# Window attention and two MLP layers: four phases over all tokens, seven block products in place of eight

## The chip, the cores and the metric

One core of one Trainium2 chip runs the whole program. The metric is the time of one execution on the device, in microseconds (us).

## The reference

Attention with 8 heads of 64 over 4 sequences of 576 tokens: each token sees itself and the 127 before it, with a linear bias per head. Its output is turned into 2304 rows of 512 and goes through two MLPs with 2048 hidden values each; the first gates with h tanh(softplus(h)) (Mish), the second with ELU.

```python
scores = scale * np.matmul(q, k.transpose(0, 1, 3, 2))
mask = (rel >= 0) & (rel < window)
scores = np.where(mask, scores + bias[None], -1000000000.0)
attn = np.exp(scores - np.max(scores, axis=-1, keepdims=True))
attn = attn / (np.sum(attn, axis=-1, keepdims=True) + 1e-09)
x = np.ascontiguousarray(np.matmul(attn, v).transpose(0, 2, 1, 3)).reshape(B * S, H * D)
h = x @ w_in                                      # layer 1
x = (h * np.tanh(np.log1p(np.exp(h)))) @ w_out
h = x @ w_in2                                     # layer 2
out = np.where(h > 0.0, h, np.exp(h) - 1.0) @ w_out2
```

Weights arrive as 64-bit floats and are made 32-bit on the chip.

## The kernel before, in words

**Products.** Every product of the layers is a sum of three products of rounded values: an operand x is split into hi (x rounded to fp32r, a copy, L411) and lo (x - hi, rounded, L421), and hi*hi + hi*lo + lo*hi are added up in one PSUM bank.

**Layer 1** runs over chunks of 512 tokens (the first in halves of 256 columns; the last 64 tokens of the four sequences form one chunk of 256). For each of 16 blocks of 128 hidden values, `hidden1` makes 12 products (L773) into a bank `ph`; Mish is taken in place (L782), split into gh and gl, and `output1` adds 12 products (L814) into banks `py`, which hold the chunk's result over all 16 blocks. The result goes to DRAM (`x2_scratch`). All weights of layer 1 stay on chip, split; those of layer 2 take their places while the last layer-1 chunk runs. **Layer 2** is the same with `hidden2` (L935), the exponential and two DVE steps for ELU (L945, L946, L948), and `output2` (L967).

**Attention** is 48 units: 4 sequences, 4 pairs of heads, 3 parts (row blocks 0 and 1; 2 and 3; the tail of 64 rows). A unit makes scores (L559 in plain fp32 for 12 units, L562 and L564 from split q and k for most others, L569 for tails), masks them (L580), takes the row maximum and the exponential (L583, L587), normalises (L603), transposes (L628), masks again (L644, L653) and multiplies with v (L679), two heads side by side in the output's partitions. Attention of the next sequence runs among the products of the current chunk.

**Weights** (`load_weights`): per 512 columns one load, two ACT and two DVE instructions and one POOL addition (L470 to L481) make 32-bit values, then hi and lo.

**What sets the order.** The program is written as a list of operations with due times; `Plan.order` walks through them with a table of costs, gives each engine the most urgent operation whose operands and buffers are ready, and may choose between ACT, DVE and POOL for copies, subtractions and scalings. The engines then run that fixed order. Where PE would wait early in the program, it puts in unused products (L349). All bulk transfers go out on the SP queue.

Of the kernel before, what the change touches and what calls it, by code (L numbers as in the profile page):

```python
# [13 lines left out]
AT = dict(lag=2, step=6.96, late=25.76, copy=1.19, both=0.34, conv=-34.61, conv1=8.2, mish=-3.26, out=-0.67,
          prep=-6.85, load=-27.75, loadr=12.24, unit=3.02, unit1=3.1, split=6.31, x2=-21.79, w2=1.86, step2=1.49,
          g=-8.44, stage=-21.52, fill=170.0, enough=1.5, u0=0.0, u1=5.67, t0=1.26, t1=11.22, t2=4.45, u2=33.61, u3=4.87,
          norma=0.5, normp=8.33, relt=-15.35, d00=-2.11, d01=-2.85, d10=0.27, d11=1.21, dx=3.28, plain=6.14,
          mm2=8.39, first=-1000.0, second=-53.57, wadd=1.47, whi=-10.73, wlo=9.29, norm=-2.13, mask=-3.68, gl=13.52,
          newton=-9.59, elu=-24.7, lead=1, turn=2.71, held=28.54, k0=8, k1=0, u4=0.0, u5=5.67)

SHIFT = dict(H18=24.6, H21=-8.7, H3=18.1, H4=12.6, H5=6.8, H69=-11.9, H7=38.3, H71=-16.6, H8=-27.9, I3=-54.8, I4=-16,
             O16=86.4, O18=56.7, O19=-34.6, O2=13.6, O4=-9.9, O5=51.4, O66=46.4, O7=19, O70=63.2, O8=-77.9, O9=35.1,
             P29=-68.1, e2=9.8, g1=-37.5, g19=-11.3, g2=-10.4, g6=-22.6, g69=1, g7=5.3, g8=104.2, u0000=-105.9,
             u0001=-69.1, u0010=-40.7, u0011=-16, u0100=-145.3, u0101=-117.5, u0102=-152.8, u0103=-153.5,
             u010l=-127.6, u0110=-11.6, u0112=11.3, u011l=-13.4, u0121=-44.7, u0122=-3.4, u012f=32.3, u012l=-77.8,
             u0131=22.6, u0201=-22.8, u0210=-9.7, u1001=3.7, u100l=-19.2, u1010=-22.3, u1011=-40.4, u101l=-24.9,
             u1020=-135.2, u1021=-51, u1022=-27.9, u1030=9, u103f=20.8, u1100=38.6, u1101=-22.4, u1103=28.6,
             u1110=-97, u1111=-137.2, u1112=-163.5, u1120=-59.6, u1121=-90.6, u1131=10.4, u1133=15.3, u113c=-62.7,
# [1021 lines left out]
```

## Time and profile before

| | us |
|---|---|
| median of 3 runs | 938.47 (935.89 to 940.75) |
| span of the profiled execution | 939.7 |
| PE busy | 924.6 (98%) |
| DVE busy | 519.1 (55%) |
| ACT busy | 499.7 (53%) |
| POOL busy | 172.6 (18%) |

The span runs from the first to the last instruction of the profiled execution; it lies inside the range of the three runs, and no other time of that execution is given. A PE duration holds the way through the array, so products of a row overlap and their starts tell the rate. A DVE or ACT duration also runs a little into the next one's when one follows at once.

### The profile page before, as it was taken

How to read it: one execution, taken by the hardware profiler on the slowest of the kernel's cores; microseconds unless marked ns; L12 is line 12 of the kernel's file. 1: busy time of each engine (PE TensorE's matmuls, PEld its weight loads, DVE VectorE, ACT ScalarE, POOL GpSimd, SP SyncE). 2: the span in 40 equal slices, each digit the busy share in tenths (PEclk: the TensorE clock that was granted, in tenths of full speed). 3: DMA queues.
4: the chain of work that ended last, by engine and by line, in shares of the span. 5: the costliest groups of instructions: out<-in, count | busy, mean ns of one | idle time of the engine just before them, and what ended most of it. 6: DMA issues, size and time to landing. Idle time of an engine off the chain costs nothing.

```text
span 939.7 us, 13784 instructions
## 1 busy us (share of the span) xinstructions
PE 924.6 (98%) x5095; PEld 773.1 (82%) x5095; DVE 519.1 (55%) x1309; ACT 499.7 (53%) x1018; POOL 172.6 (18%) x151
## 2 busy tenths in 40 slices
PE   8989999999999999999999999999999999999998
PEld 5778889987888787799888888888888888888897
DVE  6878889866524367851566894343334333333333
ACT  4888988875726567872677773233223222322232
POOL 1553455511100001010465462000000000000000
PEclk9999999999999999999999999999999999999999
DMA  9335455243202123440544440011001000100010
GB/s 218 120 127 168 161 166 173 86 126 114 86 1 85 43 65 96 130 155 13 155 146 155 149 157 24 0 45 45 1 1 56 12 1 1 45 1 0 1 46 23
DMA packets 32387, 75.08 MB, mean 80 GB/s; under 512 B 5696, under 2 KB 12352, under 8 KB 32320
## 3 DMA queue, kind: packets, MB, share of 16 engines
q1 hardware_dynamic: 31792, 73.55, 25.1%
q10 hardware_dynamic: 528, 0.66, 0.3%
q8 instruction: 40, 0.66, 0.3%
q14 instruction: 27, 0.22, 0.1%
HBM read 64.23 MB, written 9.96 MB: 79 GB/s over the span
## 4 chain that ended last, share of the span: by engine, by line
PE 88%; ACT 4%; DVE 3%; DMA 2%; POOL 1%; issue 1%; SPq 0%; POOLq 0%
PE ph L935 21%; PE py L967 21%; PE py L814 19%; PE ph L773 19%; PE ps_o L679 3%; DMA raw<-in_w_dram 2%; PE ps_t L628 1%; PE ps_s L559 1%; PE ps_s L564 1%; PE ps_s L562 1%; POOL bits L481 1%; ACT p L587 1%; ACT raw L476 1%; ACT raw L473 1%; PE ps_s L569 1%
## 5 line engine op out<-in xcount | busy, mean ns | idle before, releaser
L421 DVE TENSOR_TENSOR gl<-ph,gh 128x512 fp32r<-128x512 f32 (+1 forms) x152 | 100.3, 660 | 161.1 <-ACT gh L411 160.5
L935 PE MATMUL ph<-x,wih 128*128 128x512 f32 (+1 forms) x640 | 181.8, 367 | 0.0
L411 ACT ACTIVATE gh<-ph 128x512 fp32r<-128x512 f32 (+1 forms) x142 | 81.1, 573 | 132.5 <-PE py L967 122.9
L773 PE MATMUL ph<-xh,wih 128*128 128x256 f32 (+1 forms) x384 | 134.4, 350 | 3.6 <-DVE gl L421 3.3
L935 PEld LDWEIGHTS ph<-x,wih 128*128 128x128 f32 x640 | 117.5, 188 | 22.6 <-DVE gl L421 0.2
L814 PE MATMUL py<-gh,woh 128*128 128x256 f32 (+1 forms) x384 | 135.1, 352 | 0.0
L814 PE MATMUL py<-gh,wol 128*128 128x256 f32 (+1 forms) x384 | 129.6, 337 | 1.1 <-POOL wol L421 0.9
L773 PE MATMUL ph<-xl,wih 128*128 128x256 f32 (+1 forms) x384 | 129.8, 338 | 0.7 <-DVE xl L421 0.7
L814 PE MATMUL py<-gl,woh 128*128 128x256 f32 (+1 forms) x384 | 129.5, 337 | 0.3 <-DVE gl L421 0.3
L773 PE MATMUL ph<-xh,wil 128*128 128x256 f32 (+1 forms) x384 | 129.5, 337 | 0.0
L935 PE MATMUL ph<-x,wil 128*128 128x512 f32 (+1 forms) x320 | 117.6, 368 | 0.0
L945 ACT ACTIVATE e<-ph 128x512 f32<-128x512 f32 (+1 forms) x80 | 44.4, 555 | 132.8 <-PE ph L935 131.9
L967 PE MATMUL py<-woh,gh 128*128 128x512 f32 x288 | 112.4, 390 | 0.0
L967 PE MATMUL py<-woh,gl 128*128 128x512 f32 x288 | 112.3, 390 | 0.0
L967 PE MATMUL py<-wol,gh 128*128 128x512 f32 x288 | 112.1, 389 | 0.0
L481 POOL TENSOR_TENSOR bits<-bits,raw 128x512 int32<-128x512 int32 x64 | 87.6, 1371 | 99.6 <-DVE bits L478 72.4
L946 DVE TENSOR_SCALAR e<-e 128x512 f32<-128x512 f32 (+1 forms) x80 | 33.3, 416 | 113.6 <-ACT e L945 113.6
L773 PEld LDWEIGHTS ph<-xh,wih 128*128 128x128 f32 x384 | 73.1, 190 | 15.6 <-DVE gl L421 4.1
L814 PEld LDWEIGHTS py<-gh,wol 128*128 128x128 f32 x384 | 72.8, 190 | 9.4 <-POOL wol L421 1.1
L814 PEld LDWEIGHTS py<-gh,woh 128*128 128x128 f32 x384 | 72.8, 190 | 8.5 <-issue 1.5
L773 PEld LDWEIGHTS ph<-xl,wih 128*128 128x128 f32 x384 | 73.2, 191 | 7.9 <-DVE xl L421 0.9
L773 PEld LDWEIGHTS ph<-xh,wil 128*128 128x128 f32 x384 | 73.1, 190 | 7.8
(104 smaller groups left out, 1499.5 us busy)
## 6 DMA issues: line engine op xcount, KB each, us to landing
raw<-in_w_dram SPq DMA_DIRECT2D x64, 512.0 KB, 4.3
qkv<-in_qkv_dram SPq DMA_DIRECT2D x12, 640.0 KB, 4.0
qkv<-in_qkv_dram SPq DMA_DIRECT2D x16, 288.0 KB, 2.9
x_scratch<-ys SPq DMA_DIRECT2D x18, 256.0 KB, 2.3
out_dram<-yo SPq DMA_DIRECT2D x18, 256.0 KB, 2.0
qkv<-in_qkv_dram SPq DMA_DIRECT2D x8, 512.0 KB, 3.6
xr<-x_scratch SPq DMA_DIRECT2D x16, 256.0 KB, 2.8
v<-in_qkv_dram SPq DMA_DIRECT2D x12, 192.0 KB, 2.6
```

Of the source, the lines that this page charges most:

```text
L411: ways = [("act", act_cost(n, sbuf), lambda: nc.scalar.activation(o(), i(), AF.Copy), 0.0), ("dve", dve_cost(n, sbuf), lambda: nc.vector.t ...
L421: both(n, lambda eng: eng.tensor_tensor(out=o(), in0=i(), in1=hi().bitcast(F32), op=ALU.subtract), reads, writes, prio, only, port=not only)
L473: act(HW, lambda raw=raw: nc.scalar.activation(raw()[:, :, 1].bitcast(F32), raw()[:, :, 1].bitcast(F32), AF.Copy, scale=2.0 ** -112), (), ...
L476: act(HW, lambda raw=raw: nc.scalar.activation(raw()[:, :, 0].bitcast(I32), raw()[:, :, 0], AF.Copy, scale=2.0 ** -29), (), [(raw, 0)], pr)
L481: gps(HW, lambda raw=raw, bits=bits: nc.gpsimd.tensor_tensor(out=bits().bitcast(I32), in0=bits().bitcast(I32), in1=raw()[:, :, 0].bitcast( ...
L679: nc.tensor.matmul(o()[j * D:(j + 1) * D, c0:c0 + math.prod(y.shape[1:])], vn()[:kr, n, j], y, start=n == 0, stop=n == nkb - 1, skip_group ...
L773: nc.tensor.matmul(ph()[:, i * n:(i + 1) * n], wt()[:, cs], xx()[:, at], start=(c == 0 and m == 0), stop=(c == KC - 1 and m == 2))
L814: nc.tensor.matmul(py()[:, k, o0:o0 + m], wt()[:, cs], gg()[:, g0:g0 + m], start=(first and a == 0 and k == 0), stop=(f == NF - 1 and a == 2),
L935: nc.tensor.matmul(ph(), wt()[:, cs], xx(), start=(c == 0 and m == 0), stop=(c == KC - 1 and m == 2))
L945: act(n, lambda: nc.scalar.activation(e(), ph(), AF.Exp), [ph], [e], t, sbuf=False, table="exp")
L946: dve(n, lambda: nc.vector.tensor_scalar(out=e(), in0=e(), scalar1=1.0, scalar2=-1.0, op0=ALU.min, op1=ALU.add), (), [e], t, fast=True)
L967: nc.tensor.matmul(py(), gg()[:, ts_], wt(), start=(f == 0 and a == 0), stop=(f == NF - 1 and a == 2))
```

## The change

The four products of the program (into and out of the hidden layer, twice) become four phases, each over all 2304 tokens: inward 1 (with attention and weight conversion beside it), outward 1, inward 2, outward 2. Hidden values go to DRAM after each inward phase (`gate0` before Mish, `gate1` after ELU) and come back in the outward phase; Mish is taken there, on blocks of 768. Each product is cut into quarters: with weight blocks A and token blocks B, seven combinations P1 to P7 of block sums replace the eight products of blocks (Strassen's scheme in Winograd's form).

- `convert` makes the weight sums S1 to S4 (four additions of 256 columns for each pair of loads). Weights of inward 1 are split at once; the other three go to DRAM as seven blocks and come back in `load_weights`, one copy and one subtraction per 512 columns. Their conversion is spread over inward 1, outward 1 and inward 2.
- `combined` makes the block differences of the token side in place, `operands` (inward) and `outward` split them: a copy of 576 or 768 elements and a subtraction of the same size for each of the seven.
- In `hidden`, a step is six products of 288 columns (inward 1) or 384 (inward 2). P1, P6, P7 and P4 follow each other on one bank, A, each adding to what the bank holds; P5 and P3 share C; P2 has B. After each step the bank is copied to SBUF or added to what is there.
- In `outward`, a step runs over all 16 hidden blocks, in pairs, into two banks; operands pass through a ring of five buffers.
- Scores are plain fp32 for all units, with the two heads in rows 0 to 63 and 64 to 127 of the array and a bank for each head; the split of q and k is gone, and one load brings q, k and v.
- The result leaves the chip transposed (512 x 2304). The order is again made by `Plan.order`, with due times that follow from the uses, and unused products early in the program, 349 of them.

```diff
-    x2d = nc.dram_tensor("x2_scratch", (P, KC, NT), F32).ap()
-    xtd = nc.dram_tensor("xtail_scratch", (P, KC, B * TAIL), F32).ap()
+    gd = [dram(f"gate{i}", NF, P, NT) for i in range(2)]
+    x2d = dram("x2", KC, P, NT)
+    wsd = {1: dram("w_out1", P, 7, NQ, HALF), 2: dram("w_in2", P, NQ, 7, HALF), 3: dram("w_out2", P, 7, NQ, HALF)}
...
+    plan.ring("h", bank[:5])
+    plan.ring("a", bank[5:])
+    plan.ring("all", bank[:8])
+    plan.ring("R", right_s[:4] + wide_s[:4])
+    plan.ring("L", right_s[4:] + wide_s[4:])
...
-                        nc.tensor.matmul(o, q2()[:D, j, qo:qo + r], k2()[:D, j, ks], start=(j == 0), stop=True,
-                                         skip_group_check=True)
-                        continue
-                    nc.tensor.matmul(o, qh()[:, j, qo:qo + r], kk()[:, j, ks], start=(j == 0), stop=False,
-                                     skip_group_check=True)
-                    nc.tensor.matmul(o, ql()[:, j, qo:qo + r], kk()[:, j, ks], start=False, stop=True,
-                                     skip_group_check=True)
+                    for n in range(2):
+                        w0 = P if part == 0 and n == 0 else 0
+                        ko = (qbs[n] - 1) * P - k0
+                        for j in range(2):
+                            rs = slice(j * D, (j + 1) * D)
+                            nc.tensor.matmul(pss[j]()[:, n, w0:2 * P], qs()[rs, n * P:(n + 1) * P], ks()[rs, ko + w0:ko + 2 * P],
+                                             start=n == 0, stop=True, skip_group_check=True)
...
+        for o, l, r, op in ((s1, a21, a22, ALU.add), (s2, s1, a11, ALU.subtract), (a21, a11, a21, ALU.subtract),
+                            (s4, a12, s2, ALU.subtract)):
+            combine(HALF, o[0], l[0], r[0], [k for k in (l[1], r[1]) if k != o[1]], [o[1]], due, op)
...
+        for step in STEPS:
+            src = combined(step, 2 * T, *cells, due)
+            t = buf(ring, (2, 2, T), F32R, "xt")
+            split(2 * T, lambda t=t: t()[:, 0], lambda t=t: t()[:, 1], src[0], list(src[1]), t, due)
...
+        if step == "P5":
+            return diff(b12, b12, b11)
+        if step == "P6":
+            return diff(b12, b22, b12)
+        if step == "P7":
+            return diff(b11, b12, b11)
+        if step == "P4":
+            return diff(b21, b21, b12)
...
+        for i, step in enumerate(STEPS):
...
+            def mm(step=step, ps=ps, w=w, wi=wi, x=ops[step]):
+                for k in range(2):
+                    cs = slice(k * P, (k + 1) * P)
+                    for m, (a, b) in enumerate(((0, 0), (0, 1), (1, 0))):
+                        nc.tensor.matmul(ps(), w()[:, a, wi, cs], x()[:, b, k], start=step in FIRST and k == 0 and m == 0,
+                                         stop=k == 1 and m == 2, skip_group_check=True)
...
+            dma(P * 2 * T * 4, lambda i=i, f=f: nc.sync.dma_start(
+                out=gd[layer][f, :, c0:c0 + 2 * T], in_=(g[i]()[:, i] if layer else g[i]()).rearrange("p a b -> p (a b)")),
+                [(g[i], i, 0), (g[i], i, 1)], [("gd", layer, f, c) for c in cs], at + span + 6)
...
+                if layer == 0:
+                    act(2 * T, lambda r=r, i=i: nc.scalar.activation(r()[:, i], r()[:, i], AF.Mish), (),
+                        [(r, i, 0), (r, i, 1)], due, table="mish")
...
+                src = combined(step, 2 * T, cell(f // 2, 0), cell(f // 2, 1), cell(f // 2 + 4, 0), cell(f // 2 + 4, 1), t)
+                at_end = layer == 0 and (ci == 0 and i == 0 or ci == 2 and i > 4)
+                x = buf("L0" if at_end else "L1" if layer and ci == 0 and i == 0 else "L", (2, 2, T), F32R, "hl")
+                split(2 * T, lambda x=x: x()[:, 0], lambda x=x: x()[:, 1], src[0], list(src[1]), x, t)
```


**Three places in the order.** PE, layer 1 in mid-program, before: `ph` is a hidden bank, `py` a result bank; xh, xl and gh, gl are the split operands, w.. the split weights.

```order
L773 MATMUL ph_4362<-xh3_3382,wih_1949 128x512
L773 MATMUL ph_4362<-xl3_3393,wih_1949 128x512
L773 MATMUL ph_4362<-xh3_3382,wil_1953 128x512
L628 MATMUL ps_t_4416<-ident_68,p_4330 128x128 x2
L562 MATMUL ps_s_4420<-kk_4271,q_4257 128x256
L564 MATMUL ps_s_4420<-kk_4271,q_4257 128x256
L562 MATMUL ps_s_4420<-kk_4271,q_4257 128x256
L564 MATMUL ps_s_4420<-kk_4271,q_4257 128x256
L814 MATMUL py_3468<-gh_4347,woh_2183 128x512
L814 MATMUL py_3468<-gl_4369,woh_2183 128x512
L814 MATMUL py_3468<-gh_4347,wol_2197 128x512
```

PE, inward 1, at the start of the last sequence, after: hA, hB, hC are the banks of one hidden pair, xt the split token blocks, w the split weight sums.

```order
L837 MATMUL hB_4272<-xt_4249,w_316 128x288 x6
L837 MATMUL hC_4185<-xt_4265,w_414 128x288 x6
L837 MATMUL hC_4241<-xt_4265,w_414 128x288 x6
L837 MATMUL hA_4123<-xt_4280,w_408 128x288 x6
L837 MATMUL hA_4209<-xt_4280,w_571 128x288 x6
L837 MATMUL hA_4123<-xt_4292,w_396 128x288 x6
L837 MATMUL hA_4209<-xt_4292,w_593 128x288 x6
L837 MATMUL hA_4352<-xt_3710,w_650 128x288 x6
L837 MATMUL hA_4123<-xt_4310,w_396 128x288 x6
L837 MATMUL hA_4209<-xt_4310,w_593 128x288 x6
```

Before, a bank gets 12 products and is then left to ACT; after, bank hA_4209 gets six, is read, gets six more two rows on, is read, and so on (its first six, P1, stand a few rows ahead), with a step of another bank between.

DVE in layer 2 before: e and ph2 are the ELU's steps, gl the lo part.

```order
L421 TENSOR_TENSOR gl_7388<-ph2_7327,gh_7383 128x512
L421 TENSOR_TENSOR gl_7411<-ph2_7352,gh_7409 128x512
L946 TENSOR_SCALAR e_7416<-e_7416 128x512
L948 SCALAR_TENSOR_TENSOR ph2_7393<-ph2_7393,e_7416 128x512
L946 TENSOR_SCALAR e_7439<-e_7439 128x512
L948 SCALAR_TENSOR_TENSOR ph2_7418<-ph2_7418,e_7439 128x512
L421 TENSOR_TENSOR gl_7454<-ph2_7393,gh_7449 128x512
```

DVE in outward 1 after: graw are the gates come back, hl the split operands, bits the conversion of the next weights.

```order
L468 TENSOR_TENSOR hl_5504<-graw_5162,hl_5504 128x768
L468 TENSOR_TENSOR graw_5219<-graw_5368,graw_5219 128x2x384
L468 TENSOR_TENSOR graw_5157<-graw_5157 128x2x384
L468 TENSOR_TENSOR hl_5521<-graw_5157,hl_5521 128x768
L468 TENSOR_TENSOR graw_5219<-graw_5219 128x2x384
L468 TENSOR_TENSOR hl_5529<-graw_5199,hl_5529 128x768
L519 TENSOR_SCALAR bits_5557<-raw_5349 128x512
L519 TENSOR_SCALAR bits_5561<-raw_5076 128x512
L468 TENSOR_TENSOR hl_5559<-graw_5219,hl_5559 128x768
L527 SCALAR_TENSOR_TENSOR bits_5557<-raw_5349,bits_5557 128x512
L527 SCALAR_TENSOR_TENSOR bits_5561<-raw_5076,bits_5561 128x512
L468 TENSOR_TENSOR hl_5579<-graw_5258,hl_5579 128x768
```

Before, three instructions of 512 serve 24 products of 512 columns; after, one or two of 768 elements serve 12 products of 384, with conversion among them.

SP at the change from layer 1 to layer 2 before: xr are the loads of layer 2, ys the stores of layer 1.

```order
L913 DMA xr_5151<-x2_scratch 128x512
L913 DMA xr_5182<-x2_scratch 128x512
L913 DMA xr_5187<-x2_scratch 128x512
L827 DMA x2_scratch<-ys_5212 128x2x256
L913 DMA xr_5228<-x2_scratch 128x512
L913 DMA xr_5246<-x2_scratch 128x512
L827 DMA x2_scratch<-ys_5237 128x2x256
L468 DMA raw_5264<-in_w2_dram 128x1024
L468 DMA raw_5284<-in_w2_dram 128x1024
```

SP at the change from inward 1 to outward 1 after.

```order
L603 DMA w_4329<-w_out1 128x512
L885 DMA graw_4337<-gate0 128x768 x2
L885 DMA graw_4340<-gate0 128x768
L869 DMA gate0<-g_4144 128x576
L885 DMA graw_4340<-gate0 128x768
L869 DMA gate0<-g_4203 128x576
L869 DMA gate0<-g_4261 128x576
L885 DMA graw_4417<-gate0 128x768
L869 DMA gate0<-g_4231 128x576
L869 DMA gate0<-g_4372 128x576
L885 DMA graw_4417<-gate0 128x768
L885 DMA graw_4483<-gate0 128x768
```

Stores of the last gates now stand in one queue with the loads of the first gates and of the new weights.

## Rows read from the trace of the kernel before

**Rows 1.** the page: busy time, share and instructions of each engine.
```profile
PE 924.6 (98%) x5095; PEld 773.1 (82%) x5095; DVE 519.1 (55%) x1309; ACT 499.7 (53%) x1018; POOL 172.6 (18%) x151
```

**Rows 2.** the page: the chain that ended last, shares of the span.
```profile
PE 88%; ACT 4%; DVE 3%; DMA 2%; POOL 1%; issue 1%; SPq 0%; POOLq 0%
```

**Rows 3.** windows: us, busy (xinstructions) per engine, PE clock, DMA share, GB/s.
```profile
60.00:140.00 80.00, 74.88 (x593) 68.26 (x594) 70.35 (x179) 71.71 (x149) 34.08 (x27) 1.00 0.49 153
140.00:220.00 80.00, 79.68 (x542) 70.10 (x541) 61.98 (x158) 61.46 (x131) 30.19 (x22) 1.00 0.42 131
```

**Rows 4.** the chain in order of time: start us, us, what.
```profile
560.95 3.40 PE py L967 x15
...
881.28 0.71 PE ph L935 x6
...
930.44 5.48 PE py L967 x24
```

**Rows 5.** groups by shape, PE, 140 to 220 us: xcount | busy us, mean ns | idle before.
```profile
L814 PE MATMUL py<-gl,woh 128*128 128x256 f32 x56 | 15.8, 283 | 0.0
...
L773 PE MATMUL ph<-xh,wih 128*128 128x512 f32 x28 | 11.7, 419 | 0.0
...
L773 PE MATMUL ph<-xh,wil 128*128 128x256 f32 x30 | 8.5, 283 | 0.0
...
L814 PE MATMUL py<-gh,woh 128*128 128x512 f32 x21 | 8.7, 416 | 0.0
...
L628 PE MATMUL ps_t<-ident,p 128*128 128x128 f32 x22 | 3.7, 271 | 0.0
```

**Rows 6.** timeline of PE, first 60 us: start us, us, engine line op.
```profile
0.84 6.23 PE L349 MATMUL unused<-const-bfloat16-1.0 128*128 128x256 bf16 x29 [0.84 <-PEq L1036]
...
28.97 1.51 PE L349 MATMUL unused<-const-bfloat16-1.0 128*128 128x256 bf16 x12
...
38.95 1.09 PE L679 MATMUL ps_o<-pt,qkv 128*64 128x128 f32 x12
...
40.34 1.99 PE L559 MATMUL ps_s<-qkv 64*128 64x256 f32 x8
```

**Rows 7.** timeline of DVE, 100 to 125 us.
```profile
115.60 0.68 DVE L421 TENSOR_TENSOR gl<-ph,gh 128x512 fp32r<-128x512 f32 x1
116.20 1.21 DVE L421 TENSOR_TENSOR q<-qkv,q 128x512 fp32r<-128x512 f32 x1
...
121.49 0.29 DVE L583 CUSTOM_DVE_ANT_0 p<-ps_s,relm 128x128 f32<-128x128 f32 x1
...
121.70 0.42 DVE L470 TENSOR_SCALAR bits<-raw 128x512 uint32<-128x512 uint32 x1
122.04 0.42 DVE L412 CAST woh<-bits 128x512 fp32r<-128x512 f32 x1
```

**Rows 8.** groups by shape, whole span: xcount | busy us, mean ns | idle before.
```profile
L478 DVE SCALAR_TENSOR_TENSOR bits<-raw,bits 128x512 uint32<-128x512 uint32 x64 | 54.2, 850 | 18.9 <-ACT raw L473 18.5
...
L421 DVE TENSOR_TENSOR wil<-bits,wih 128x512 fp32r<-128x512 f32 x23 | 28.2, 1228 | 7.8 <-ACT wih L411 6.5 <-PE py L814 1.0
...
L421 DVE TENSOR_TENSOR x<-xr,x 128x512 fp32r<-128x512 f32 x9 | 6.2, 698 | 6.4 <-ACT x L411 6.2
```

**Rows 9.** timeline from 558 us (POOL beside DVE), and the POOL group.
```profile
558.80 1.48 POOL L421 TENSOR_TENSOR x<-xr,x 128x512 fp32r<-128x512 f32 x1
559.04 1.51 DVE L470 TENSOR_SCALAR bits<-raw 128x512 uint32<-128x512 uint32 x1
...
L481 POOL TENSOR_TENSOR bits<-bits,raw 128x512 int32<-128x512 int32 x64 | 87.6, 1371 | 99.6 <-DVE bits L478 72.4 <-DVE st L598 10.2 <-issue 7.0
```

**Rows 10.** the page: DMA share and GB/s in 40 slices; transfers issued.
```profile
DMA  9335455243202123440544440011001000100010
GB/s 218 120 127 168 161 166 173 86 126 114 86 1 85 43 65 96 130 155 13 155 146 155 149 157 24 0 45 45 1 1 56 12 1 1 45 1 0 1 46 23
...
xr<-x_scratch SPq DMA_DIRECT2D x16, 256.0 KB, 2.8
```

More of the change, by code (lines that the diff above doesn't have):

```diff
@@ L11 @@
 BF16 = mybir.dt.bfloat16
[L14 to L28, printed above, removed]
-             u2001=-8.8, u2003=-6.8, u2012=-86.1, u2024=12.6, u2031=-18, u203c=-6.7, v10_0=9, v10_1=4.5, v12_1=-51.1,
-             v15_1=-14.2, w0_0=-41.9, w1_0=-17.8, w1_1=38.7, w2_1=6.1, w3_1=-41.6, w4_0=9.1, w4_1=-50.5, w5_0=25.5,
-             w5_1=-107.2, w6_0=-18.3, w6_1=45.2, w7_1=20.3, w8_1=13.6, z00=-43.7, z01=9.1)
 F32R = mybir.dt.float32r
@@ L250, in order @@
         if None in done:
-            raise RuntimeError(f"{done.count(None)} operations are never ready")
+            raise RuntimeError(f"{done.count(None)} operations are never ready, the first is {ops[done.index(None)]['group']}")
         self.span = max(done)
@@ L269, in room, with take, over @@
     @staticmethod
-    def room(b, t):
+    def take(b):
+        if not b.taken:
+            b.taken = True
+            b.slot.pos += 1
+    @staticmethod
+    def over(b, t):
+        return b.taken and b.left == 0 and b.free_at <= t + 1e-9
+    def room(self, b, t):
         if b.taken:
             return True
-        r = b.ring
-        if b.seq != r["next"]:
-            return False
-        if b.seq < r["slots"]:
-            return True
-        old = r["bufs"][b.seq - r["slots"]]
-        return old.left == 0 and old.free_at <= t + 1e-9
+        s = b.slot
+        if s.queue[s.pos] is not b:
+            return False
+        if s.pos:
+            return self.over(s.queue[s.pos - 1], t)
+        return all(self.over(x.queue[-1], t) for x in s.zone.get("after", ()) if x.queue)
 def mm_cost(n):
@@ L427, in compare, with split, vec @@
+    def split(n, hi, lo, src, key, into, due):
+        copy(n, hi, src, key, [(into, 0)], due)
+        combine(n, lo, src, lambda: hi().bitcast(F32), key + [(into, 0)], [(into, 1)], due)
+    def vec(emit, reads, writes, due):
+        dve(P, emit, reads, writes, due, fast=True)
     def compare(o, i, op):
@@ new lines, in convert @@
+    def convert(w, q, due, into=None):
+        outward, names = w % 2, ("A11", "A12", "A21", "A22")
+        src = wd[w // 2]
+        tiles = []
+        for f in (q, q + NQ):
+            raw, bits = buf("raw", (DM, 2), U32, "raw"), buf("bits", (DM,), U32, "bits")
+            s = src[f, :, 2 * outward * DM:2 * (outward + 1) * DM]
+            dma(P * DM * 8, lambda raw=raw, s=s: nc.sync.dma_start(out=raw().rearrange("p n w -> p (n w)"), in_=s),
+                (), [(raw, 0), (raw, 1)], due)
+            dve(DM, lambda raw=raw, bits=bits: nc.vector.tensor_scalar(
@@ L488, in load_weights @@
-        plan.group = None
-    xc_of, x_of, ended = {}, {}, set()
-    def unit(b, pr, part, t0, dt, banks, first=None):
+                [(raw, 1)], [bits], due, port=True)
+            plan.op([("pool", pool_cost(DM), lambda raw=raw, bits=bits: nc.gpsimd.tensor_tensor(
+                out=bits().bitcast(I32), in0=bits().bitcast(I32), in1=raw()[:, :, 0].bitcast(I32), op=ALU.add), 0.0)],
+                [(raw, 0)], [bits, (bits, 0), (bits, 1)], due=due)
+            tiles.append(bits)
+        x, y = tiles
```

1076 lines of the change are left out of this document (542 added, 534 removed).

## Prediction

> **What bounds the kernel now.** I read the page's engine line first, then its chain. TensorE (PE) is busy 98% of a 939.7 us span [rows 1], and PE makes up 88% of the chain that ended last [rows 2]; VectorE (DVE) and ScalarE (ACT) stand at 55% and 53%. Next, windows, since those shares are means: from 60 to 140 us, where attention, weight conversion and the first layer share the engines, DVE is busy 70.35 of 80 us and PE 74.88; from 140 to 220, DVE 61.98 and PE 79.68 [rows 3]. So PE is the bound, and only where DVE is nearly full does PE idle: 5.4 of those 160 us, 3.4%. A change that takes products away pays in PE time, as long as DVE, which gets the additions in exchange, doesn't come up to PE.
>
> PE's rate: 15 products of 512 columns take 3.40 us on the chain, 0.2267 each; six of 256 take 0.71, 0.1183 each [rows 4]. On the line through both, 288 columns cost 0.1319 and 384 cost 0.1725.
>
> **PE after the change, term by term.** Before, the layers are 2784 products of 512 columns and 1344 of 256: 631 + 159 = 790 us. After, the program holds 1344 of 288 columns in the first inward phase (H1) and 1008 of 384 in each of the phases outward 1, inward 2, outward 2 (O1, H2, O2): 177.2 + 3 x 173.9 = 699 us. This is 7/8 of the columns and a little more fixed cost per product, a gain of 91 us.
>
> Attention. From 140 to 220 us PE ran 84 + 61 products of 512 columns and 90 + 167 of 256 (three operand forms each, one row of each shown) and 22 transposes [rows 5]: 145 x 0.2267 + 257 x 0.1183 = 63.3 of the 79.7 busy us, so 16.4 us for the attention around 22 transposes, 0.745 each with scores, value products and switching. The transposes stay 144: 107.3 us, if the new scores cost what the split ones do. A row pair shown nowhere in this trace has these bounds: eight records of the unpaired 64-row score (1024 columns) take 1.99 us, and the value products, which pair the two heads on the output side, 1.09 us for 1024 columns [rows 6]. The split form takes eight products of 256, 0.95 us. I take the paired price, since that row is of the same data type and also of two heads side by side; it adds 0.1 us in 32 units, too little to count.
>
> Start. 29 unused products at the cold rate end at 7.1 us, as now. The new order holds 320 more while the first batch's attention runs alone and PE waits for DVE; at 1.51 us for 12, 0.12 each [rows 6], they are 38.4 us that PE does execute. They stand for the idle time of the start, so I count them and no idle time there.
>
> H1 = 7.1 + 38.4 + 107.3 + 177.2 = 330.0 us; with the other phases 330.0 + 521.7 = 851.7.
>
> **DVE, the cover for all this.** Back to back, a 512-element subtraction starts the next instruction after 0.60 us, a 128-element score reduction after 0.21, a fast 512-element one after 0.34 [rows 7]: about 1.02 ns per element plus 0.08, so 0.86 for 768, 0.47 for 384, 0.37 for 288, 0.34 for 256. The other end is the recorded duration, 0.698 for 512 [rows 8], 16% more. Counted from the new order:
> - O1: 84 operand subtractions and 48 block differences of 768 (113.5), 33 weight subtractions (20), x operands (8.6), 15 sums of 288 and 19 of 384 (14.5), conversion (8), small ones: 167 us, 194 by durations, against 174 of PE.
> - H2: 168 sums and gate steps of 384 (79), 95 fast ones (26), weights (14), x operands (19), nine conversion pairs (28): 166, 193 by durations.
> - O2: 140, 163. H1: about 250, 291, against 330.
>
> I take the low ends, because a loaded engine runs back to back. On top comes GpSimd (POOL): a fast DVE instruction of 0.34 us took 1.51 us beside a POOL one of 1.48 [rows 9]. Against 0.698 the 23 subtractions wil lost 0.53 us each and the 64 shifts 0.15 [rows 8], 22 us beside 172.6 us of POOL [rows 1]. At twice that share, POOL's 48 us in O1 and H2 (27 conversion adds at 1.37 [rows 9] and some 11 us of sums) cost DVE about 6 us per phase: 173 and 172. So in O1 and H2 DVE and PE are level, 87% DVE on the whole. I price that by the 3.4% of PE idle that rows 3 show at 83% DVE: on H1 after its first 72 us (258) and on O1 and H2 (348), 606 x 0.034 = 20.6 us. Below, this term ends at nothing.
>
> The Trainium skill has a rule that speaks against the change: SBUF — State Buffer, section "SBUF: two separate sides", says that DVE and GpSimd share one port pair under an exclusive lock, so that a DVE instruction with two SBUF inputs and a GpSimd one never run together and the later waits out the earlier. Nearly all added DVE work is of that kind. Rows 9 agree in the one case; what full blocking would give is the fourth rival.
>
> **DMA and handovers.** The order moves 186.6 MB: 73.7, 37.3, 44.3 and 31.3 by phase, over 330, 174, 174 and 174 us: 223, 214, 255 and 180 GB/s. Shown are 218 GB/s at nine tenths of the engines in the first slice and 161 to 173 at four to five tenths [rows 10]. The first slice is the attention's small pieces, which become rows of at least 2.3 KB; by the other slices there is room, so no time. All of it stays on SP's one queue, now 536 transfers: a store that waits for its gate holds up the loads behind it, weight tiles and the next raw blocks, and PE is who waits in the end. At a handover, at worst the load (2.8 us [rows 10]), the rounding copy (about 0.6) and the subtraction (0.7 [rows 8]) lie bare, 4.1 us; at best none, since the order mixes the first products of the next phase into the end of the last. I take 3 each, 9 us. The end stays as it is: last products begin at 930.44 and take 5.48 [rows 4], 3.8 us before the span's end.
>
> ACT gets the copies out of PSUM and loses its table changes between exp and Mish, since no gate runs beside attention any more; I price it at nothing, below DVE in every phase. If it is late with those copies, the third rival tells the cost.
>
> **Sum.** 851.7 + 20.6 + 9 + 3.8 = 885.1 on a profiled span of 939.7, which lies 1.2 over the median of the runs and within their range (935.89 to 940.75): 884.
>
> **Rivals.**
> 1. PE alone sets the time, and buffers of five operands hide every difference: 884 - 20.6 - 9 = 854. For it: from 140 to 220 us PE idles 0.3 of 80 us at 77% DVE [rows 3]. Against: no stretch shown has DVE over 88%.
> 2. Row pairs don't run together: per unit 1.99 - 0.95 = 1.04 us for row blocks 2 and 3 and 0.76 for 0 and 1, in 24 units behind the start: 884 + 22 = 906. Against: the paired value products.
> 3. Slower: the accumulating banks. A step of six products on a bank that holds an earlier result (P6, P7, P4 on A, P3 on C) can't begin before ACT or DVE has read the bank, and the PE queue stands meanwhile. There are 4 x 56 = 224 such steps. Cover is one to three other steps of 0.79 to 1.04 us; the read takes 0.4 to 0.5 us by the line of rows 7 and may stand behind one or two instructions of 0.6. At 0.22 us bare per step this eats 50 us and the gain is gone; at 0.35 it is 78, less the 10 or so in it that the idle term holds already: 951. For it: 80 to 95% loads on both reading engines. Against: the order puts other steps between.
> 4. Full blocking by POOL: 48 us of POOL work in O1 and H2 lengthen DVE by 24 us each, to 191 and 190, both over PE: 884 + 17 + 16 = 917.
> 5. Transfers cap at 218 GB/s: H1 338, H2 203 in place of 330 and 174: 884 + 8 + 29 = 921.
>
> **How the numbers follow.** Forecast 884 with its own range 865 to 903: 0.50. Rival 1 0.15, 2 0.07, 3 0.10, 4 0.10, 5 0.08. The range must hold 8 in 10 and takes in all but rival 3 and the far side of 1 and 5: 848 to 932. A change of under 0.5% (934 to 943) can't be told from none here; some of rivals 3 and 5 falls in it. Faster 0.87, within 0.04, slower 0.09.
>
> **What would show it.** H1 ends near 340 us (first product of outward 1 by then, first of inward 1 near 55); each later phase takes 175 to 190; DVE busy 85% or more in O1 and H2 and lower in O2, with PE's small waits ending on DVE. Rival 2: paired scores near 2 us per unit. Rival 3: PE waits on ACT or DVE that end at copies out of h banks. Rival 4: long DVE instructions beside POOL. Rival 5: DMA share at nine tenths and waits on DMA. I am wrong if the front lasts far over 60 us, or if an outward phase takes over 200.

## The result, and the profile after

The changed kernel takes **890.71 us** (median of 4 runs, 890.05 to 894.79) against 938.06 for the kernel before beside it (4 runs, 935.89 to 940.75): a ratio of 0.950, 95% interval 0.947 to 0.953. The forecast was 884, range 848 to 932. The profiled execution took 890.05 us, its span is 888.3.

The page of the changed kernel, the lines that answer to [rows 1] and [rows 2]: busy time and share of each engine, the transfers, and the chain that ended last by engine.

```profile
PE 864.1 (97%) x5597; PEld 816.9 (92%) x5597; DVE 786.3 (89%) x1780; ACT 576.7 (65%) x1270; POOL 171.8 (19%) x140
...
DMA packets 85969, 187.70 MB, mean 211 GB/s; under 512 B 8576, under 2 KB 30080, under 8 KB 85888
...
PE 80%; DVE 10%; DMA 4%; issue 3%; ACT 2%; POOL 1%; SPq 0%; POOLq 0%; ACTq 0%; DVEq 0%
```

PE is still the bound, but VectorE went from 55% to 89%, and PE's part of the chain from 88 to 80%: a fifth of the new chain is other engines' work, transfers and issue time. The next view is the windows by phase, as [rows 3]: inward 1 behind the front, outward 1, inward 2, outward 2. Behind the stretch stand PE, weight load, DVE, ACT and POOL with busy us and instructions, then the granted clock, the transfers' share and GB/s.

```profile
0.00:58.00 58.00, 56.66 (x495) 44.95 (x496) 48.26 (x215) 41.36 (x134) 22.14 (x26) 1.00 0.50 167
58.00:330.00 272.00, 265.48 (x2080) 235.13 (x2077) 243.59 (x808) 196.41 (x582) 70.39 (x58) 1.00 0.70 234
330.00:504.00 174.00, 171.95 (x975) 171.06 (x975) 159.37 (x194) 132.57 (x195) 39.10 (x25) 1.00 0.68 232
504.00:690.00 186.00, 183.58 (x1033) 182.47 (x1032) 181.76 (x372) 121.35 (x240) 40.20 (x31) 0.99 0.70 239
690.00:888.30 198.30, 186.42 (x1023) 183.27 (x1021) 153.32 (x195) 85.04 (x121) 0.00 (x0) 0.97 0.42 149
```

DVE is 92% busy in outward 1 and 98% in inward 2, and still PE idles only 2.1 and 2.4 us there. The loss is in the last line: 11.9 us of PE idle, 8.1 of it before 735 us and 3.3 behind the last product. PE's timeline around the change from inward 2 (L837) to outward 2 (L912) shows it; in brackets stands PE's wait ahead of the group and what ended it.

```profile
692.10 1.32 PE L837 MATMUL hA<-xt,w 128*128 128x384 f32 x6 [0.65 <-DVE g L468]
694.74 0.44 PE L912 MATMUL oA<-hl,w 128*128 128x384 f32 x1 [1.32 <-ACT hl L463]
697.70 9.29 PE L912 MATMUL oA<-hl,w 128*128 128x384 f32 x35 [2.52 <-DVE hl L468]
708.73 0.44 PE L912 MATMUL oC<-hl,w 128*128 128x384 f32 x1 [1.73 <-ACT hl L463]
709.85 3.22 PE L912 MATMUL oC<-hl,w 128*128 128x384 f32 x11 [0.69 <-DVE hl L468]
712.87 2.82 PE L912 MATMUL oA<-hl,w 128*128 128x384 f32 x12
...
727.63 2.17 PE L912 MATMUL oA<-hl,w 128*128 128x384 f32 x11 [1.24 <-DVE hl L468]
```

The waits for the operands of outward 2 (`hl`) add up to 7.5 us. Between them 35 products take 9.29 us in place of 6.3. The windows of that stretch say why: in the first the granted clock is 0.51, near the lower of its two levels (1.2 of 2.4 GHz), right behind the gaps. The transfers stand at 402 to 410 GB/s.

```profile
698.00:704.00 6.00, 6.00 (x20) 6.00 (x20) 6.00 (x10) 0.84 (x1) 0.00 (x0) 0.51 1.05 409
704.00:710.00 6.00, 3.58 (x19) 2.85 (x18) 5.46 (x7) 3.77 (x5) 0.00 (x0) 1.00 1.03 410
710.00:716.00 6.00, 6.00 (x26) 6.00 (x27) 2.50 (x4) 0.28 (x1) 0.00 (x0) 0.72 1.05 402
```

### The profile page after: what moved, and what is told of

Read it like the earlier page. It is cut to its first block, busy times and chain, and to the rows that moved or that the text cites. A ratio compares the mean times of both kernels' runs of the same rounds, so it can differ in the third digit from the quotient of the medians.

```text
span 888.3 us, 16116 instructions
## 1 busy us (share of the span) xinstructions
PE 864.1 (97%) x5597; PEld 816.9 (92%) x5597; DVE 786.3 (89%) x1780; ACT 576.7 (65%) x1270; POOL 171.8 (19%) x140
## 4 chain that ended last, share of the span: by engine, by line
PE 80%; DVE 10%; DMA 4%; issue 3%; ACT 2%; POOL 1%; SPq 0%; POOLq 0%; ACTq 0%; DVEq 0%
PE hA L837 20%; PE oA L912 18%; PE hC L837 10%; PE oC L912 10%; PE hB L837 5%; PE unused L423 5%; PE oB L912 4%; PE ps_o L748 3%; PE ps_s L648 3%; DVE hl L468 3%; PE ps_t L703 2%; DVE w L468 2%; DVE graw L468 1%; DMA w_out<-bits 1%; DMA raw<-in_w_dram 1%
## 5 line engine op out<-in xcount | busy, mean ns | idle before, releaser
L837 PE MATMUL hA<-xt,w 128*128 128x288 f32 (+1 forms) x1344 | 236.0, 318 | 3.5 <-DVE g L468 2.7
L463 ACT ACTIVATE hl<-graw 128x768 fp32r<-128x768 f32 x162 | 136.3, 845 | 138.2 <-PE oA L912 79.4
L912 PE MATMUL oA<-hl,w 128*128 128x384 f32 x1152 | 216.8, 342 | 5.2 <-DVE hl L468 3.8
L837 PEld LDWEIGHTS hA<-xt,w 128*128 128x128 f32 x1344 | 208.7, 189 | 8.9 <-DVE g L468 3.3
L912 PEld LDWEIGHTS oA<-hl,w 128*128 128x128 f32 x1152 | 206.4, 191 | 6.7 <-DVE hl L468 5.1
L468 DVE TENSOR_TENSOR hl<-graw,hl 128x768 fp32r<-128x768 f32 x168 | 167.0, 1000 | 41.8 <-ACT hl L463 40.4
L837 PE MATMUL hC<-xt,w 128*128 128x288 f32 (+1 forms) x672 | 122.0, 318 | 0.4 <-DVE xt L468 0.4
L912 PE MATMUL oC<-hl,w 128*128 128x384 f32 x576 | 109.6, 341 | 4.3 <-ACT hl L463 2.7
L837 PEld LDWEIGHTS hC<-xt,w 128*128 128x128 f32 x672 | 105.7, 189 | 2.5 <-DVE xt L468 1.0
L912 PEld LDWEIGHTS oC<-hl,w 128*128 128x128 f32 x576 | 102.5, 189 | 5.8 <-ACT hl L463 3.3
L837 PE MATMUL hB<-xt,w 128*128 128x288 f32 (+1 forms) x336 | 61.7, 318 | 1.5 <-ACT g L463 0.9
L837 PEld LDWEIGHTS hB<-xt,w 128*128 128x128 f32 x336 | 52.7, 188 | 2.8 <-ACT g L463 1.7
L912 PE MATMUL oB<-hl,w 128*128 128x384 f32 x288 | 53.8, 338 | 0.0
L912 PEld LDWEIGHTS oB<-hl,w 128*128 128x128 f32 x288 | 50.9, 188 | 0.0
```

Source lines behind the costliest of these rows:

```text
L463: ways = [("act", act_cost(n, sbuf), lambda: nc.scalar.activation(o(), i(), AF.Copy), 0.0), ("dve", dve_cost(n, sbuf), lambda: nc.vector.t ...
L468: emit = lambda eng: eng.tensor_tensor(out=o(), in0=x(), in1=y(), op=op)
L837: nc.tensor.matmul(ps(), w()[:, a, wi, cs], x()[:, b, k], start=step in FIRST and k == 0 and m == 0, stop=k == 1 and m == 2, skip_group_ch ...
L912: nc.tensor.matmul(bk[name, d](), w()[:, a, wi, cs], x()[:, b, k], start=step in FIRST and f + k == 0 and m == 0, stop=f + k == NQ - 1 and ...
```

## Experiments

The changed kernel was run again beside some of them, as their measure:

> The changed kernel itself once more, on the chip on which the three others of this set run: 890 us, as the measure that their few microseconds are held against. Every theory expects 888 to 895.

It took 892.28 us, ratio to before 0.9487 (0.9473 to 0.9501); its profiled span is 891.7, 3.4 us longer than that of the first execution. Ratios below are all to the kernel before on the same chip, spans are of the profiled executions.

### Eight products in place of seven

All four phases and the paired scores stay; the scheme goes, and with it three of every seven splits of operands and weights and 19 of 187 MB of transfers. (One due-time constant, `chunk`, follows the longer phases.)

```
-STEPS = ("P1", "P5", "P6", "P2", "P7", "P3", "P4")
-ORDER = ("A11", "S1", "S2", "A12", "S3", "S4", "A22")
+STEPS = ("P1", "P5", "P2", "P6", "P3", "P7", "P4", "P8")
+ORDER = ("A11", "A21", "A12", "A22", "A11", "A21", "A12", "A22")
...
-        for o, l, r, op in ((s1, a21, a22, ALU.add), (s2, s1, a11, ALU.subtract), ...
...
-            src = combined(step, 2 * T, *cells, due)
+            src = b[name]
```

> All four phases, the middle values via DRAM and the row-paired scores stay, but each layer's quarter blocks are multiplied as eight plain products in place of seven: no sums and differences of blocks or weights, 5376 products against 4704. The 672 more are 192 of 288 columns at 0.1333 us and 480 of 384 columns at 0.176 us, 25.6 + 84.5 = 110 us. Theory A (TensorE is the bound and the seven-product scheme's extra work lies beside it): 890 + 110 less the 7 us of gaps that a relieved VectorE no longer makes, 985 to 1005, slower than the kernel before it all. Rival (VectorE and the transfers set the time of the seven-product phases, so that the eighth product is nearly free): 890 to 930.

The count in this expectation is wrong: there are 4992 products against 4368, 624 more, 192 of 288 columns and 432 of 384. At the rates named there that is 25.6 + 76.0 = 101.6 us, and theory A becomes 977 to 997.

Measured: 962.62 us, ratio 1.0235 (1.022 to 1.0251), **slower than the kernel before**, and between the theories: neither holds. The page's engine line and windows (front, inward 1, outward 1, inward 2, outward 2):

```profile
PE 949.2 (99%) x6162; PEld 909.1 (95%) x6162; DVE 486.6 (51%) x1301; ACT 436.2 (45%) x997; POOL 92.0 (10%) x74
...
58.00:350.00 292.00, 286.47 (x2236) 258.85 (x2233) 202.62 (x708) 196.97 (x570) 60.58 (x43) 0.99 0.77 255
350.00:545.00 195.00, 195.00 (x1113) 195.00 (x1112) 79.07 (x104) 94.70 (x133) 18.57 (x13) 1.00 0.55 184
545.00:750.00 205.00, 205.00 (x1167) 205.00 (x1166) 100.42 (x207) 62.26 (x118) 0.00 (x0) 1.00 0.35 127
750.00:960.00 210.00, 207.89 (x1185) 207.57 (x1184) 54.08 (x67) 45.80 (x61) 0.00 (x0) 1.00 0.32 107
```

So the seven-product scheme is worth 962.6 - 892.3 = 70 us of the 101.6 that its products take away, and the phases with the new attention cost 22 us. Without the scheme PE has no idle time behind 350 us, the change into outward 2 included, and DVE is half empty: the 31 us that are missing are what the scheme's further work gives back, additions, splits and transfers together; this run doesn't part them. The first outward product starts at 350.5 us here and at 332.0 with seven, 18.5 of 25.6 us kept; behind it 559.7 us against 611.0, 51 of 76 kept. Most of the loss, 25 us, therefore lies in the last three phases. By an estimate, what the phases cost is products of fewer columns: at 0.1333 us for 288 columns and 0.1758 for 384 (3456 products in 607.5 us here), the 1.77 million columns take 812 us, where the kernel before, with products of 512 and 256, takes 790 by the prediction's sum. That is the whole 22 us, but attention changed as well, so it isn't shown apart.

### Do the paired scores run together?

First the order alone: both products of one head, then both of the other.

```
-                    for n in range(2):
+                    for js, n in itertools.product(range(2), range(2)):
...
-                        for j in range(2):
+                        for j in (js,):
```

> The score products of the two heads of a pair are no longer alternated: both of one head, then both of the other, the same products and bytes. Theory A (the alternated ones run together on the two halves of the rows, 1.07 us for eight records of 256 columns): a unit's scores take up to twice as long, some 0.5 us more for each of 32 units, so 16 us more, 900 to 908 where TensorE is busy beside them. Rival (they do not run together, or their time is hidden behind VectorE): 889 to 893.

Measured: 891.91 us, ratio 0.948 (0.9465 to 0.9496), no difference. It says nothing against pairing: a unit's eight records (four products, two records each) still took 1.14 us, as with alternation. The question was therefore put to the rows themselves: both heads on rows 0 to 63.

```
-                            rs = slice(j * D, (j + 1) * D)
+                            rs = slice(0, D)
```

> Both heads' score products read rows 0 to 63 of q and k (the second head gets the first one's scores, so the output is not the reference's); count, sizes and order stay. Theory A (the two heads' products run together because they stand on different halves of the rows, in whichever order they are written): eight records of 256 columns take 1.9 to 2.0 us as in the kernel before, in place of 1.06, and the 32 units together some 25 us more; where the front of 58 us is bound by other work part of it is hidden, so 905 to 918 us. Rival 1 (they are faster for another reason than the rows): 1.06 us and 890 to 894. Rival 2 (they take twice as long, but behind VectorE's 90% in inward 1): 1.9 us and 890 to 897.

Measured: 913.61 us, ratio 0.9724 (0.97 to 0.9748), 22 us slower. The timeline's row of one unit's scores in the changed kernel (run again), with the heads one after the other, and on the same rows:

```profile
112.05 1.14 PE L648 MATMUL ps_s<-qkv 64*128 64x256 f32 x8
```

```profile
112.25 1.14 PE L648 MATMUL ps_s<-qkv 64*128 64x256 f32 x8
```

```profile
120.06 1.99 PE L648 MATMUL ps_s<-qkv 64*128 64x256 f32 x8
```

The last is the 1.99 us of [rows 6]. The two halves of the rows do work at the same time, in either order: in the traces a unit's records start in pairs, 3 to 7 ns apart with alternation and 12 to 14 ns with one head after the other, and on the same rows never less than 111 ns apart. It is worth 22 us, nearly all in inward 1: the first outward product starts at 353.3 us in place of 332.0. Theory A of this run holds; theory A of the run before had the pairing right and the part of the order wrong.

### GpSimd beside VectorE

```
-AT = dict(copy=1.11, both0=-0.71, both1=-7.5, both2=-2.92, ...
+AT = dict(copy=1.11, both0=-0.71, both1=-0.71, both2=-2.92, ...
```

> In the outward phases GpSimd may take differences and low parts of blocks much sooner (its handicap against VectorE in the ordering goes from 7.5 to 0.71 us); the work itself is the same. Theory A (a GpSimd operation of 1.5 us beside VectorE holds VectorE up by about as much as it takes off it): 888 to 895, no gain. Rival 1 (it relieves VectorE, whose late operands make the gaps): 880 to 887. Rival 2 (GpSimd's blocking costs more than the work it takes): 896 to 915.

Measured: 925.96 us, ratio 0.9841 (0.9819 to 0.9862), 34 us slower than the changed kernel: rival 2 in kind, and beyond its 915. The engine line, and the groups of the low part of an operand (on DVE) and of block differences and weights (now on POOL):

```profile
PE 879.0 (95%) x5597; PEld 822.0 (89%) x5597; DVE 831.4 (90%) x1655; ACT 581.8 (63%) x1279; POOL 413.2 (45%) x256
...
L468 DVE TENSOR_TENSOR hl<-graw,hl 128x768 fp32r<-128x768 f32 x161 | 251.5, 1596 | 34.5 <-ACT hl L463 33.9
...
L468 POOL TENSOR_TENSOR graw<-graw 128x768 f32<-128x768 f32 x53 | 130.7, 2477 | 93.3 <-DVE graw L468 47.2
...
L468 POOL TENSOR_TENSOR w<-w 128x512 fp32r<-128x512 f32 x59 | 100.0, 1708 | 61.5 <-DVE w L464 31.4
```

The same group in the changed kernel, run again:

```profile
L468 DVE TENSOR_TENSOR hl<-graw,hl 128x768 fp32r<-128x768 f32 x168 | 169.2, 1014 | 41.6 <-ACT hl L463 40.5
```

POOL has 241 us more work in 116 more instructions. DVE has 125 instructions fewer and is busy 43 us longer. The 53 block differences and 59 weight subtractions would have taken DVE 53 x 0.980 + 59 x 0.723 = 95 us; in place of falling by that it rose by 43, so 241 us of POOL held DVE up for some 138 us, 0.57 us per us. The 241 us hold POOL's own waits too: its shortest 768-element difference took 1.84 us and its shortest 512-element subtraction 1.28, and by such shortest times some 60 of the 241 are waits, which makes the price about 0.76 us per us of POOL's own work, an estimate. The low parts show it one by one: 101 with a POOL instruction beside them took 1.98 us on the mean, 60 without one 0.95. PE's waits in this run end on DVE and ACT, none on POOL. So the fourth rival's mechanism is there, and the changed kernel escapes it because its planner keeps POOL out of those additions. The Trainium skill states the lock (SBUF — State Buffer, "SBUF: two separate sides"); this run agrees in kind, since the instructions of both engines get longer side by side.

### The stall ahead of outward 2: buffers and clock

The raw blocks of outward 2 get buffers that inward 2 doesn't hold to its end, and its split operands pass through another ring:

```
-    plan.ring("L1", wide_s[4:])
+    plan.ring("R1", wide_s[4:] + right_s[:4] + wide_s[:2])
+    plan.ring("L1", right_s[4:] + wide_s[3:4] + wide_s[2:3])
...
-        raws = [buf("R", (2, 2, T), F32, "graw") for f in range(NQ)]
+        raws = [buf("R1" if layer else "R", (2, 2, T), F32, "graw") for f in range(NQ)]
...
-                x = buf("L0" if at_end else "L1" if layer and ci == 0 and i == 0 else "L", (2, 2, T), F32R, "hl")
+                x = buf("L0" if at_end else "L1" if layer else "L", (2, 2, T), F32R, "hl")
```

> The raw blocks of outward 2 get buffers that inward 2 does not hold to its end, so the loads of the first of them may start before inward 2's last products; nothing else is changed. Theory A (the stall behind inward 2 is loads that wait for buffers held by inward 2's operands): the idle 7.5 us and the 4.2 us at a lower clock between 692 and 735 us mostly go, so 879 to 884. Theory B (the loads stand at the ceiling of the transfers, 402 to 410 GB/s, whichever buffer they go to): 888 to 891, the stall stays or moves. Theory C (earlier loads collide with what inward 2's end moves and delay its products): 891 to 900.

Measured: 894.96 us, ratio 0.9513 (0.9495 to 0.953): not faster. PE's timeline, the groups behind a wait:

```profile
694.66 0.44 PE L913 MATMUL oA<-hl,w 128*128 128x384 f32 x1 [1.31 <-ACT hl L464]
698.65 3.89 PE L913 MATMUL oA<-hl,w 128*128 128x384 f32 x11 [3.55 <-DVE hl L469]
718.63 4.64 PE L913 MATMUL oA<-hl,w 128*128 128x384 f32 x12 [5.06 <-ACT w L464]
```

The wait didn't go, part of it moved from raw blocks to weight tiles, 5.06 us for `w` where there was none, under transfers of 372 to 398 GB/s from 702 to 720 us. Theory A falls. Theory C has the number, 891 to 900, but not the reason: the last product of inward 2 ended at 693.4 us, as in the first execution of the changed kernel. The stall moved, as theory B says, at a price that B didn't have. Other buffers alone don't help; that whichever load goes first makes the other late fits this run, but isn't shown by it.

Unused products in the gaps from 600 us on:

```
-                        if e != "pe" or t > self.fill[2]:
+                        if e != "pe" or self.fill[2] < t < 600:
...
-                for b in bufs:
+                for b in sorted(bufs, key=lambda b: b.slot.tag):
```

> Unused products may stand in TensorE's idle gaps from 600 us on, as they do before 90 us; loads and waits stay. Theory A (after the gap at 693 to 710 us the granted clock falls to 0.51 to 0.72 and stretches the next products by some 4 us): with the gaps filled the clock stays at 1.00 and the time falls by 2 to 4, to 887 to 889. Rival (the first products behind the gap wait for their operands anyway, a higher clock only makes them wait longer): 890 to 892, no change.

> Both edits together: other buffers for the raw blocks of outward 2, and unused products in the gaps from 600 us on. If waits and clock are two separate losses: the sum of both single gains, 875 to 882. If the clock falls only because of the waits, and the other buffers end these: no better than with the other buffers alone, within 2 us of it.

Measured: 892.68 (ratio 0.9486, 0.9472 to 0.9499) and 895.21 (0.9521, 0.9501 to 0.954). Both tell little: the planner's own table sees almost no gap there, and put in ten unused products more (5607 records against 5597), with the other buffers five (5602), so the clock was hardly touched and neither theory was put to the test. What the clock costs is read from the two executions of the changed kernel: in the first, 35 products in 9.29 us, 11 in 3.22 and 12 in 2.82, where as many take some 6.3, 2.2 and 2.3 at the full clock, 4.5 us in all; in the second, 24 products in 6.00 in place of 4.4, 1.6 us. It is 2 to 5 us, and not the same each time. The second's row:

```profile
702.68 6.00 PE L912 MATMUL oA<-hl,w 128*128 128x384 f32 x24 [2.52 <-DVE hl L468]
```

### The conversion of the last weights

The second outward weights are converted while inward 2 ends (568 to 689 us). Left out:

```
-            for w in (1, 2, 3):
+            for w in (1, 2):
...
+        w = min(w, 2) if w % 2 == 0 else 1
         d, outward = wsd[w], w % 2
```

> The conversion of the second outward weights is left out (its loads, VectorE, ScalarE and GpSimd work, and its stores, some 70 to 80 us of work spread over the end of inward 2); outward 2 multiplies the first layer's outward weights in its place, so the output is not the reference's. Theory A (a VectorE that is 98% busy in inward 2 is what makes TensorE's small waits there, 2.4 us of 186, and the dips at 634 to 646 us): 885 to 888. Rival 1 (TensorE alone sets the time, all of it lies beside): 889 to 892. Rival 2 (VectorE is the true bound of inward 2, TensorE's busy time hides it): 860 to 880.

Then with its transfers back, but not its arithmetic:

> Of the conversion of the second outward weights only the transfers stay: the raw words are loaded and stored in the same blocks and sizes, with no VectorE, ScalarE and GpSimd work between; outward 2 multiplies the first layer's outward weights, but still waits for these stores, so the output is not the reference's. Leaving the whole conversion out brought the ratio to before from 0.9487 to 0.9336, about 14 us. Theory A (what cost the 14 us is VectorE's share of the conversion, some 30 us in a phase where it is 98% busy): nearly the same as without it all, 876 to 883 us, ratio 0.933 to 0.939. Theory B (the 16 MB of transfers and their places in SyncE's queue ahead of the loads of outward 2): 888 to 893, ratio 0.945 to 0.950. Between the two: both have a part.

```
+            if w < 3:
+                dve(DM, lambda raw=raw, bits=bits: nc.vector.tensor_scalar(
...
+        if w == 3:
...
+            parts = [(d[:, 0:2, q], tiles[0], "A11 S3"), (d[:, 2:4, q], tiles[1], "A12 A22"), (d[:, 4:7, q], tiles[0], "S1 S2 S4")]
...
+        d, outward = wsd[1 if w == 3 else w], w % 2
```

Measured: 878.29 us without it (ratio 0.9336, 0.9317 to 0.9355), 887.14 with the transfers alone (0.9439, 0.9421 to 0.9458). Windows of the end of inward 2 and of the change into outward 2, of the changed kernel run again, of transfers alone, and of neither:

```profile
640.00:690.00 50.00, 46.32 (x259) 45.29 (x260) 48.08 (x111) 32.54 (x67) 11.06 (x9) 1.00 0.84 288
690.00:735.00 45.00, 35.78 (x186) 33.67 (x185) 40.49 (x62) 21.04 (x35) 2.90 (x3) 0.96 0.82 299
```

```profile
640.00:690.00 50.00, 50.00 (x287) 49.93 (x286) 42.71 (x97) 30.76 (x64) 0.00 (x0) 1.00 0.90 308
690.00:735.00 45.00, 37.87 (x185) 36.25 (x184) 37.59 (x52) 25.42 (x40) 0.00 (x0) 0.89 0.58 217
```

```profile
640.00:690.00 50.00, 50.00 (x286) 50.00 (x286) 47.19 (x104) 34.93 (x71) 0.00 (x0) 1.00 0.80 263
690.00:735.00 45.00, 41.55 (x232) 39.84 (x231) 43.05 (x59) 24.82 (x37) 0.00 (x0) 1.00 0.63 231
```

Both theories have a part, and the parts lie in different places. By the ratios the arithmetic is 4.5 us and the transfers 9.7, each good to some 2 us; by the spans, 891.7, 885.0 and 877.0, it is 6.7 and 8.0.

The arithmetic costs time before the end of inward 2. From the first product of outward 1 to the end of inward 2's last one it is 366.4 us in the changed kernel run again (364.1 in its first execution) and 359.9 with the transfers alone, 4 to 6.5 us less: PE has no idle time from 504 to 690 us there, and 4.2 with the arithmetic (2.4 in the first execution).

The transfers cost their time behind it. PE's groups behind a wait or at a low clock, first with transfers alone, then with neither:

```profile
693.22 0.45 PE L916 MATMUL oA<-hl,w 128*128 128x384 f32 x1 [1.69 <-ACT hl L463]
695.90 7.86 PE L916 MATMUL oA<-hl,w 128*128 128x384 f32 x35 [2.24 <-DVE hl L468]
705.48 0.44 PE L916 MATMUL oC<-hl,w 128*128 128x384 f32 x1 [1.73 <-ACT hl L463]
706.61 3.89 PE L916 MATMUL oC<-hl,w 128*128 128x384 f32 x11 [0.69 <-DVE hl L468]
710.30 3.42 PE L916 MATMUL oA<-hl,w 128*128 128x384 f32 x12
```

```profile
694.06 2.37 PE L913 MATMUL oA<-hl,w 128*128 128x384 f32 x12 [0.35 <-DVE hl L468]
697.86 2.20 PE L913 MATMUL oA<-hl,w 128*128 128x384 f32 x11 [1.44 <-DVE hl L468]
700.54 4.29 PE L913 MATMUL oC<-hl,w 128*128 128x384 f32 x23 [0.29 <-DVE hl L468]
708.29 2.38 PE L913 MATMUL oA<-hl,w 128*128 128x384 f32 x12 [1.37 <-ACT y L463]
```

With the transfers alone the change into outward 2 costs what it costs in the changed kernel: 7.1 us of waits (0.78 of it at 727 us) and some 4.4 at the lower clock, 11.5 in all, against 12.0 in the changed kernel's first execution and 10.2 in its second. With neither it costs 3.5 us, and the granted clock stays at 1.00. What differs is how much is still to be loaded: of the 28 weight tiles of outward 2, 17 are issued behind 690 us in the changed kernel, 12 with transfers alone and 3 with neither, and the transfers stand near 400 GB/s until 726, 714 and 708 us. With neither, the order changes too: outward 2's weight loads no longer have to follow stores, and 13 of its products stand ahead of inward 2's last step. The runs don't part the bytes from that order.

The expectation of rival 2 for the first run, 860 to 880, holds in size, but not in cause: DVE at 98% is not the bound of inward 2 as a whole, it is late at its end only, and most of the 14 us are transfers.

That pointed to a version that might beat both kernels: half of this conversion moved forward into outward 1.

```
                 best = o["due"]
+            if o["group"] in ("c30", "c31", "c32", "c33"):
+                best = min(best, 470 + 5 * int(o["group"][2]))
```

> Half of the conversion of the second outward weights (four of eight blocks) is due near 470 us, in outward 1 where VectorE is 92% busy, in place of the end of inward 2 where it is 98% busy. Theory A (VectorE at 98% at the end of inward 2 makes the stalls at 638 to 650 us and late loads behind 693 us): 6 to 10 us of the 14 come back, 882 to 887 us, ratio to before 0.938 to 0.943. Rival (VectorE has no room in outward 1 either, the stalls only move forward): 890 to 896.

Measured: 900.01 us, ratio 0.9578 (0.9551 to 0.9606), 8 us slower, the rival in kind and beyond its 896. The windows of the end of outward 1 and the start of inward 2, then of the end of inward 2:

```profile
450.00:504.00 54.00, 49.68 (x263) 48.11 (x261) 53.40 (x67) 43.41 (x67) 17.92 (x9) 0.94 0.82 289
504.00:560.00 56.00, 51.99 (x279) 50.26 (x280) 50.47 (x93) 36.65 (x66) 18.69 (x6) 0.97 0.76 262
...
640.00:690.00 50.00, 50.00 (x286) 50.00 (x285) 48.58 (x99) 35.72 (x71) 9.40 (x9) 1.00 0.67 221
```

The end of inward 2 is mended, 50.00 of 50, and 8.3 us are lost from 450 to 560, where DVE goes to 99% in the first of the two stretches (0.6 us in the changed kernel). Of the waits there 4.6 us end on DVE and 3.8 on ACT. There was no room for this work at the place that was tried; others weren't tried. No version here with the whole computation in it is faster than the changed kernel beyond the noise.

## Why the prediction was right

The signs, the bound and the size were right: 884 against 890.7. By its own steps, in the span of the first profiled execution (885.1 summed, 888.3 measured); the third row begins at the end of inward 2's last product, 693.4 us:

| stretch | predicted | measured |
|---|---|---|
| to the first product of outward 1 | 338.8 | 329.3 |
| outward 1 and inward 2 | 365.6 | 364.1 |
| outward 2 and end | 180.7 | 194.9 |

- **Rates.** 288 columns cost 0.1333 us, not 0.1319; 384 cost 0.1767 (six in 1.06), not 0.1725. The line through 256 and 512 was 1 to 2% low: some 14 us in all (4 us in each of the three phases of 384, 2 in inward 1).
- **Inward 1.** The first inward product came at 58.0 us (55 expected). PE's idle time behind it, 6.5 us, is near the 8.8 that its share of the idle term allows. Products took 179 us, so start, unused products and attention took 144 where 153 were summed. The 349 unused products kept PE busy for 45.4 us, as summed, so the rest of [rows 5] (0.745 per transpose) was some 9 us too dear; which part of attention was cheaper isn't settled.
- **Idle time beside a full DVE.** 11.8 us were allowed in outward 1 and inward 2; from 330 to 690 us PE idled 4.5. The 3.4% of [rows 3] was too much for these phases, though DVE was fuller there (92 and 98%) than in the rows it was taken from (83%); here PE's idle time doesn't follow DVE's share. The surplus paid for the rates.
- **DVE.** Its load was well seen in sum: 159 us in outward 1 and 182 in inward 2, 341 where 173 and 172 were taken; outward 1 lies under the count's low end, 167, inward 2 between its ends, 166 and 193.
- **The handovers, the mis-sized term.** 3 us each were taken. Into outward 1 and inward 2 that was enough (1.5 and 0.6 us of waits); into outward 2 it was some 12: 7.5 us of waits and 4.5 at the lower clock. The step that failed is the bound that at worst one load, one copy and one subtraction lie bare, 4.1 us. Several operands in a row came late, because the transfers of the last weights' conversion, the loads of outward 2's weight tiles and its first raw blocks fall together: with the conversion's transfers alone 11.5 us are still there, without them (and the order that they bring) 3.5 are left, close to the 3 that were taken. The lower clock behind the waits stands nowhere in the sum.
- **Luck.** The terms miss by more than the total does: rates and this handover cost some 23 us more than summed, attention and the idle terms some 19 less. And the span was turned into a time by taking 1.2 us off; every run's time lies 1.7 to 2.0 above its span (890.05 against 888.3), so 885.1 stands for 887. The forecast's mechanism holds, but part of the number's nearness is chance.
- **The five rivals.** PE alone (854): PE idles 24 us of the span, and the change into outward 2 alone costs 12, so no. Rows that don't pair (906): they pair, and without pairing it is 913.6. Accumulating banks (951): waits for reads of `h` banks are single ones, the longest 2.05 us, so no. Full blocking by POOL (917): DVE's mean for a 768-element low part is 1.00 us with the planner's choice; but the mechanism is strong, 926 as soon as POOL is let in. (The DVE instruction of [rows 9] reads one SBUF operand; instructions with two are shown beside POOL by the run above.) Transfers capped at 218 GB/s (921): the phases moved 232 to 239 GB/s on the mean and over 400 at the peak, so no; but transfers make the loss at the one place where the peak stands.

## What to carry to other kernels

Taking an eighth of the products away pays as long as another engine has room for the additions; here, where that engine went from half to nine tenths, about a third of the gain went back, some 12 of the 31 us at one place, where the next phase's loads fall on the last one's end. Price a handover by everything that is due in the tens of microseconds ahead of it (stores and loads above all), not by one load and one copy. And when work is moved off a place where an engine is full, look first whether the place where it goes has room: here VectorE was 92% busy there, and moving it cost 8 us.

## What was not expected of the hardware

- Two fp32 score products on different halves of the rows run at the same time even where both of one head stand ahead of both of the other: 1.14 us for eight records in either order, 1.99 on the same half; the records of the two heads start within 14 ns of each other.
- The core's transfers reached 412 GB/s over six microseconds, nearly twice the 218 GB/s that the kernel before showed in its first slice [rows 10].
- 241 us of GpSimd work on SBUF operands made VectorE some 138 us longer, and were themselves slow: 2.48 us on the mean, 1.84 at the least, for a 768-element difference that takes VectorE 0.98.
